# Two-tile experts with six units of lag in one shared pair buffer, four units converted ahead, and copies of turned rows ahead of conversions

## The chip, the cores and the metric

The kernel runs on one core of a Trainium2 chip. The metric is the device time of one execution in microseconds (us), taken as the median of several runs. Engines are called as in the profile: PE is TensorE (PEld its weight loads, PEldq the part of PE that reads the program in order and puts weight loads and matmuls into its queue, here called the sequencer), DVE is VectorE, ACT is ScalarE, POOL is GpSimd, SP is SyncE.

## What is computed

Three layers follow one another, all in float32: a retention attention over 8 heads (2 x 768 tokens), a dense layer of two matmuls with a leaky maximum between them (512 to 2048 to 512), and a layer of eight experts, in which each of the 1536 tokens goes to one expert. The change touches the third layer alone:

```python
def _moe2_ref(x, w_gate, w1, w2, capacity):
    N, D = x.shape                        # 1536, 512
    E = w_gate.shape[1]                   # 8
    logits = x @ w_gate
    expert_idx = np.argmax(logits, axis=1)
    ...
    disp = np.zeros((E, capacity, D), dtype=np.float32)    # capacity 384
    for i in range(N):
        e = expert_idx[i]
        if counts[e] < capacity:
            disp[e, counts[e]] = x[i]
            pos[i] = counts[e]
            counts[e] += 1
            keep[i] = True
    h = np.maximum(np.einsum('ecd,edf->ecf', disp, w1), 0.0)
    y = np.einsum('ecf,efd->ecd', h, w2)
    for i in range(N):
        if keep[i]:
            out[i] = gate_w[i] * y[expert_idx[i], pos[i]]
```

## The kernel before, in words

**The stage that the change touches.** The attention and the dense layer fill the span up to about 346 us, the experts the rest. The experts run one after the other. Each expert's 1024 hidden columns are cut into `PF` = 8 units of 128. A unit `u` holds 512 KB of weights: its part of w1 (columns 0 to 511 of the buffer) and its part of w2 (columns 512 to 1023). `refill` loads a unit's buffer (`land`, `xland`) on SP's queue long before its use.

**Classes.** How many tokens an expert has is known only at run time. `by_class` compares the count in a register with 128 and 256 and branches, so the program holds the code of an expert three times: for one, two or three tiles of 128 tokens. With the inputs of this case the eight experts have 144, 384, 35, 77, 80, 27, 183 and 384 tokens; so experts 0 and 6 are of class 2, experts 1 and 7 of class 3, and experts 2 to 5 of class 1. At the end of an expert every engine branches to the code of the next one's class (L1080 and L1081). `name_next` (L838) tells the sequencer ahead of time which way the first of these branches goes.

**One expert.** `expert` runs over steps `i`. In a step it computes the hidden columns of unit `i` on PE (`mm_h`: for classes 2 and 3 twelve matmuls, since each float32 operand stands as a high and a low part; for class 1 four matmuls on the operands as they are). `ew_h` then takes the relu from PSUM: ACT writes the high part `gh` (L746), DVE the low part `gl` (L747). `mm_y` (L756) multiplies the hidden columns of unit `i - lag` with w2 and sums in PSUM: three matmuls for a tile of tokens. `LAGS` says how many units the hidden columns are ahead of these products: 8, 4 and 2 for classes 1, 2 and 3.

**Conversions.** `conv` makes the high part (`hi`, ACT, L726) and the low part (`lo`, DVE, L727) of a unit's weights. For class 1 only the w2 half is needed (128x512), for the other classes both halves (128x1024). The list `todo` holds what is converted during an expert: its own units but the first two, which were converted in the expert before it (four ahead of expert 0), and at the end the first two of the next expert, at full width because the next class isn't known yet. A conversion is issued behind each `ew_h`, as far as buffers are free.

**The next expert's rows.** `load_x` gathers an expert's token rows by an indirect DMA on POOL. `prep_x` turns them: PE transposes into PSUM (L653), then ACT and DVE copy them to SBUF as high and low parts (`cxh`, L656, and `cxl`, L660), or for class 1 as plain halves (`cxf`, L664 and L671). In step `PREP[cls]` (8, 5, 4) the turn is issued first, then the next gather, then `mm_h`, `mm_y` and the conversion of that step, and the copies last. All of it goes through `by_class`, since the next expert's class decides the number of tiles.

## Time and profile before

| what | value |
|---|---|
| median of 3 runs | 539.44 us (537.92 to 539.96) |
| the profiled execution's own time | 537.16 us |
| its span in the profile | 535.4 us |
| PE busy (matmuls) | 514.8 us, 96% of the span |
| DVE busy | 329.4 us, 62% |
| ACT busy | 234.2 us, 44% |
| POOL busy | 39.5 us, 7% |
| mean granted clock of PE | 0.99 |

The span runs from the first instruction to the last; 1.76 us of the profiled execution's time lie around it. The shares are means over stages. PE's matmuls are pipelined, so two of them overlap in the records and a group's distance from start to start is what it costs, not its duration.

### The profile page before, as it was taken

The numbers are of one execution on the slowest core, as the hardware profiler recorded it, in microseconds if no ns is written. First come the engines' busy times: TensorE is split into PE (matmuls) and PEld (weight loads), VectorE is DVE, ScalarE is ACT, GpSimd is POOL, SyncE is SP. The second block draws the span as 40 slices with busy tenths as digits, with TensorE's granted clock in tenths as the row PEclk, the third lists the DMA queues.
The fourth block names the chain that finished last, engine by engine and source line by source line (L and its number), as shares of the span: only waits on it lengthen the run. The fifth ranks groups of instructions, "written<-read, shape, count | busy, mean of one in ns | idle before, by whom it ended". The sixth has DMA issues, their size and how long they took to land.

```text
span 535.4 us, 8754 instructions
## 1 busy us (share of the span) xinstructions
PE 514.8 (96%) x3279; PEld 460.2 (86%) x3281; DVE 329.4 (62%) x636; ACT 234.2 (44%) x485; POOL 39.5 (7%) x66
## 2 busy tenths in 40 slices
PE   7899999999999999999999999899799999998995
PEld 4888989999999999999999998588798899986894
DVE  3999993379689649947735254553343666655430
ACT  1887973354344325423422231252333566654421
POOL 0000000000000000000001012411101212201002
PEclk9999999999999999999999999989899999999998
DMA  8987781022334602410411313463451999910001
GB/s 318 376 271 253 238 260 58 1 80 78 99 105 151 196 2 78 122 38 5 153 65 75 137 59 119 134 227 103 111 164 46 372 339 354 366 72 13 21 1 60
DMA packets 23783, 76.54 MB, mean 143 GB/s; under 512 B 3578, under 2 KB 3706, under 8 KB 23712
## 3 DMA queue, kind: packets, MB, share of 16 engines
q1 hardware_dynamic: 21312, 70.26, 37.9%
q0 software_dynamic: 2400, 5.39, 2.9%
q8 instruction: 38, 0.62, 0.5%
q14 instruction: 33, 0.27, 0.2%
HBM read 68.15 MB, written 9.96 MB: 146 GB/s over the span
## 4 chain that ended last, share of the span: by engine, by line
PE 61%; DMA 24%; issue 10%; DVE 2%; POOL 1%; ACT 1%; POOLq 1%; DVEq 0%
PE ps_h L369 25%; DMA xr<-x2d,gix 24%; PE ps_y L420 18%; PE ps_a L420 7%; PE ps_a L251 2%; PE ps_a L185 2%; PE ps_a L469 2%; PE ps_a L240 2%; PE ps_a L456 1%; PE ps_h L223 1%; PE ps_y L888 1%; DVE am L207 0%; POOL xr L638 0%; POOL out L850 0%; PE ps_a L597 0%
## 5 line engine op out<-in xcount | busy, mean ns | idle before, releaser
L376 ACT ACTIVATE hs<-ps_h 128x384 f32<-128x384 f32 x64 | 31.4, 490 | 106.0 <-PE ps_h L369 106.0
L381 DVE SCALAR_TENSOR_TENSOR hs<-hs 128x384 f32<-128x384 f32 x64 | 35.6, 556 | 67.5 <-ACT hs L376 67.5
L420 PE MATMUL ps_y<-hi,gh 128*128 128x512 f32 x138 | 56.3, 408 | 0.0
L369 PE MATMUL ps_h<-xh,hi 128*128 128x384 f32 x256 | 55.7, 339 | 0.0
L369 PE MATMUL ps_h<-xl,hi 128*128 128x384 f32 x256 | 54.8, 336 | 0.0
L369 PE MATMUL ps_h<-xh,lo 128*128 128x384 f32 x256 | 54.7, 336 | 0.0
L420 PE MATMUL ps_y<-lo,gh 128*128 128x512 f32 x138 | 54.0, 391 | 0.0
L420 PE MATMUL ps_y<-hi,gl 128*128 128x512 f32 x138 | 54.0, 391 | 0.0
L385 ACT ACTIVATE gh<-hs 128x384 fp32r<-128x384 f32 x64 | 33.6, 526 | 45.0 <-DVE hs L381 45.0
L369 PEld LDWEIGHTS ps_h<-xh,hi 128*128 128x128 f32 x256 | 46.0, 188 | 4.8
L391 DVE TENSOR_TENSOR gl<-hs,gh 128x384 fp32r<-128x384 f32 x64 | 35.6, 556 | 21.3 <-ACT gh L385 21.3
L747 DVE SCALAR_TENSOR_TENSOR gl<-ps_h,gh 128x384 fp32r<-128x384 f32 (+2 forms) x44 | 18.5, 421 | 48.7 <-ACT gh L746 41.8
L369 PEld LDWEIGHTS ps_h<-xl,hi 128*128 128x128 f32 x256 | 45.3, 188 | 0.0
L369 PEld LDWEIGHTS ps_h<-xh,lo 128*128 128x128 f32 x256 | 45.0, 188 | 0.0
L756 PE MATMUL ps_y<-hi,gh 128*128 128x512 f32 x112 | 44.2, 395 | 0.0
L756 PE MATMUL ps_y<-hi,gl 128*128 128x512 f32 x112 | 43.9, 392 | 0.0
L756 PE MATMUL ps_y<-lo,gh 128*128 128x512 f32 x112 | 43.8, 391 | 0.0
L746 ACT ACTIVATE gh<-ps_h 128x384 fp32r<-128x384 f32 (+2 forms) x44 | 16.9, 385 | 56.8 <-PE ps_h L705 45.2
L727 DVE TENSOR_TENSOR lo<-xland,hi 128x1024 fp32r<-128x1024 f32 (+1 forms) x32 | 32.7, 1023 | 9.3 <-ACT hi L726 9.1
L727 DVE TENSOR_TENSOR lo<-land,hi 128x1024 fp32r<-128x1024 f32 (+1 forms) x28 | 27.9, 995 | 8.5 <-ACT hi L726 6.1
L420 PEld LDWEIGHTS ps_y<-hi,gl 128*128 128x128 f32 x138 | 25.9, 188 | 5.6
L420 PEld LDWEIGHTS ps_y<-hi,gh 128*128 128x128 f32 x138 | 26.0, 188 | 4.3 <-issue 0.3
(162 smaller groups left out, 964.9 us busy)
## 6 DMA issues: line engine op xcount, KB each, us to landing
land<-wc SPq DMA_DIRECT2D x32, 512.0 KB, 4.3
xland<-wc SPq DMA_DIRECT2D x32, 512.0 KB, 4.3
land<-wb SPq DMA_DIRECT2D x31, 512.0 KB, 5.0
land<-qkv SPq DMA_DIRECT2D x19, 512.0 KB, 5.6
out<-zero SPq DMA_DIRECT2D x12, 256.0 KB, 6.4
x2d<-rows SPq DMA_DIRECT2D x12, 256.0 KB, 2.1
early<-qkv SPq DMA_DIRECT2D x5, 512.0 KB
cst<-cst_in SPq DMA_DIRECT2D x1, 512.0 KB
```

Of the source, the lines that this page charges most:

```text
L185: nc.tensor.matmul(out=at["s", c][h2][:, a, :], lhsT=kT[r, a, :], rhs=qT[r, a, :], start=True, stop=True)
L240: nc.tensor.matmul(out=y_ps[:, a, :], lhsT=at["t", c - 1][:, a, :], rhs=at["q", c][:, a, :], start=(a == 0), stop=False, skip_group_check= ...
L369: nc.tensor.matmul(out=h_ps, lhsT=w[i][:, dc * P:(dc + 1) * P], rhs=x[j][:, dc, :], start=(n == 0), stop=(n == 3 * KD - 1))
L376: nc.scalar.activation(out=hs, in_=gt[u][0], func=ACTF.Copy)
L381: nc.vector.scalar_tensor_tensor(out=hs, in0=hs, scalar=0.01, in1=hs, op0=ALU.mult, op1=ALU.max)
L385: nc.scalar.activation(out=gh, in_=gt[u][0], func=ACTF.Copy)
L391: nc.vector.tensor_tensor(out=gl, in0=hs, in1=gh.bitcast(F32), op=ALU.subtract)
L420: nc.tensor.matmul(out=yb[ti][t], lhsT=gt[u][i][:, t * P:(t + 1) * P], rhs=w[j][:, 512:1024], start=(f == fs[0] and n == 0), stop=(f == fs ...
L727: nc.vector.tensor_tensor(out=lo[:, o], in0=src[:, o], in1=hi[:, o].bitcast(F32), op=ALU.subtract)
L746: nc.scalar.activation(out=gh, in_=hp, func=ACTF.Relu)
L747: nc.vector.scalar_tensor_tensor(out=gl, in0=hp, scalar=0.0, in1=gh.bitcast(F32), op0=ALU.max, op1=ALU.subtract)
L756: nc.tensor.matmul(out=yps[t], lhsT=gg[i][:, t * P:(t + 1) * P], rhs=w[j][:, 512:1024], start=(k == 0 and n == 0), stop=(k == PF - 1 and n ...
```

## The change

Five things are changed in the expert stage:

1. **Buffers.** The relu's outputs of all classes (and the pairs of the dense layer, which come earlier) live in one tile `pairs`, cut by class: 8 pairs of 128 columns, 6 of 256 (the last three quarter-buffers in a tile `more` that reuses the dense layer's `sums`), or 4 of 384. `h_of` uses all free PSUM banks of a class.
2. **Lag.** Class 2 runs six units ahead instead of four (`LAGS`).
3. **`AHEAD`.** Four units of the next expert are converted during an expert, at full width, instead of two.
4. **Place of the copies.** The copies of the turned rows are issued right behind the turn and the gather, ahead of the step's `mm_h`, `mm_y` and conversion. `PREP` becomes 8, 8, 5 and `NAME` 4, 8, 8.
5. **Form of the branches in `prep_x`.** The first tile is turned without a question; a second and a third inside nested `If`s without an `Else`. The copies are asked in two nested steps.

```diff
@@ -94,7 +94,9 @@
-    g_p = ctx.enter_context(tc.tile_pool(name="g", bufs=3))
+    g_p = ctx.enter_context(tc.tile_pool(name="g", bufs=1))
+    pairs = g_p.tile([P, 6 * BW], FR, name="pairs")
+    sums = g_p.tile([P, 2 * BW], F32, tag="sums", name="hs")
...
@@ -659,35 +666,47 @@
-        def high(cls):
-            if cls == 1:
-                nc.scalar.activation(out=f[:, 0:2, :], in_=tps[0][:, 0:2, :], func=ACTF.Copy)
-                return
-            for t in range(cls):
+        def high(ts):
+            for t in ts:
                 hi1(t)
 
-        def low(cls):
-            if cls == 1:
-                nc.vector.tensor_copy(out=f[:, 2:KD, :], in_=tps[0][:, 2:KD, :])
-                return
-            for t in range(cls):
+        def low(ts):
+            for t in ts:
                 lo1(t)
...
-        by_class(s, 0, lambda cls: [turn(t) for t in range(cls)])
+        def half(e):
+            if e == ENGS[1]:
+                nc.scalar.activation(out=f[:, 0:2, :], in_=tps[0][:, 0:2, :], func=ACTF.Copy)
+            else:
+                nc.vector.tensor_copy(out=f[:, 2:KD, :], in_=tps[0][:, 2:KD, :])
+
+        turn(0)
+        with tc.If(over(s, ENGS[0], 1)):
+            turn(1)
+            with tc.If(over(s, ENGS[0], 2)):
+                turn(2)
         yield
-        by_class(s, 1, high)
-        by_class(s, 2, low)
+        for e, fn in ((ENGS[1], high), (ENGS[2], low)):
+            with tc.If(over(s, e, 1)) as many:
+                fn((0, 1))
+                with tc.If(over(s, e, 2)):
+                    fn((2,))
+            with many.Else():
+                half(e)
         yield
...
@@ -726,19 +744,25 @@
-    LAGS = {1: PF, 2: 4, 3: 2}
-    PREP = {1: 8, 2: 5, 3: 4}
-    NAME = {1: 4, 2: 9, 3: 8}
+    LAGS = {1: PF, 2: 6, 3: 2}
+    PREP = {1: 8, 2: 8, 3: 5}
+    NAME = {1: 4, 2: 8, 3: 8}
+    AHEAD = 4
     every = []
 
     def h_of(u, cls):
-        banks = (hps + yps[cls:])[:5 - cls]
+        banks = hps + yps[cls:]
         i = u % PF // len(banks) % (4 // (cls + cls % 2))
         return banks[u % PF % len(banks)][:, i * cls * P:(i + 1) * cls * P]
 
+    more = []
+
     def g_of(u, cls):
-        i = u // 4 % 2 if cls == 1 else 0
-        return [x[:, i * P:(i + cls) * P] for x in gpair[u % 4]]
+        i = u % PF % {1: 8, 2: 6, 3: 4}[cls]
+        w = cls * P
+        n = 6 * BW // w
+        return [pairs[:, j * w:(j + 1) * w] if j < n else more[0][:, (j - n) * w:(j - n + 1) * w]
+                for j in (2 * i, 2 * i + 1)]
...
@@ -764,8 +788,8 @@
-        todo = [(u, cls) for u in range(u0 + (4 if s == 0 else 2), u0 + PF)]
-        todo += [(u, 2) for u in range(u0 + PF, min(NU, u0 + PF + 2))]
+        todo = [(u, cls) for u in range(u0 + AHEAD, u0 + PF)]
+        todo += [(u, 2) for u in range(u0 + PF, min(NU, u0 + PF + AHEAD))]
...
@@ -800,6 +823,7 @@
                 step(xg)
                 if s + 2 < NS:
                     load_x(s + 2)
+                step(xg)
             h = hidden(i) if i < PF else None
...
-            if i == PREP[cls] and xg is not None:
-                finish_all(xg)
             refills(i)
```

The first place at which instructions move is PE's program in a class 1 expert, at the turn of the next expert's rows, between its hidden columns and its first products. Before, the turn stands there three times, once for each class; these are the copies for two tiles and for one, and the products behind them (the rows are in the program's order; which of them run is decided by the branches):

```order
L629 COMPARE_AND_BRANCH
L653 MATMUL ps_a<-cst,xr 128x128 [waits DMASW3_49]
L653 MATMUL ps_a<-cst,xr 128x128 x3
L653 MATMUL ps_a<-cst,xr 128x128 [waits DMASW4_49,DMASW6_49,DMASW2_49,DMASW0_49]
L653 MATMUL ps_a<-cst,xr 128x128 x3
L629 UNCONDITIONAL_BRANCH
L653 MATMUL ps_a<-cst,xr 128x128 [waits DMASW3_49]
L653 MATMUL ps_a<-cst,xr 128x128 x3
L629 UNCONDITIONAL_BRANCH
L756 MATMUL ps_y<-hi,gh 128x512 [waits Activation_49]
L756 MATMUL ps_y<-lo,gh 128x512
L756 MATMUL ps_y<-hi,gl 128x512
```

In the changed kernel the same place reads:

```order
L660 MATMUL ps_a<-cst,xr 128x128 [waits DMASW3_49]
L660 MATMUL ps_a<-cst,xr 128x128 x3
L698 COMPARE_AND_BRANCH
L660 MATMUL ps_a<-cst,xr 128x128 [waits DMASW4_49,DMASW6_49,DMASW2_49,DMASW0_49]
L660 MATMUL ps_a<-cst,xr 128x128 x3
L700 COMPARE_AND_BRANCH
L660 MATMUL ps_a<-cst,xr 128x128 [waits DMASW7_49,DMASW5_49,DMASW1_49]
L660 MATMUL ps_a<-cst,xr 128x128 x3
L700 UNCONDITIONAL_BRANCH
L700 UNCONDITIONAL_BRANCH [waits PE_49]
L698 UNCONDITIONAL_BRANCH [waits PE_49]
L780 MATMUL ps_y<-hi,pairs 128x512 [waits Activation_49]
```

The turn of one tile stands once, ahead of the question. On the side of an `If` that does nothing there is now a branch that waits for PE's own semaphore (`PE_49`, which PE's matmuls raise when they are done), that is, for the transposes just issued. It is run through where the next expert is of class 1 (the row with L698) and where it is of class 2 (L700), not where it is of class 3.

The second place is DVE's program at the end of a class 1 expert. Before (`gl` is the relu's low part, `lo` a converted weight, `cxl` and `cxf` copies of turned rows):

```order
L727 TENSOR_TENSOR lo<-xland,hi 128x1024 [waits DMAHW4_49,Activation_49]
L626 COMPARE_AND_BRANCH
L660 TENSOR_TENSOR cxl<-ps_a,cxh 128x4x128 [waits Activation_49,Pool_49]
L660 TENSOR_TENSOR cxl<-ps_a,cxh 128x4x128 x2
L626 UNCONDITIONAL_BRANCH
L629 COMPARE_AND_BRANCH
L660 TENSOR_TENSOR cxl<-ps_a,cxh 128x4x128 [waits Activation_49,Pool_49]
L660 TENSOR_TENSOR cxl<-ps_a,cxh 128x4x128
L629 UNCONDITIONAL_BRANCH
L671 COPY cxf<-ps_a 128x256 [waits Activation_49]
L629 UNCONDITIONAL_BRANCH
L727 TENSOR_TENSOR lo<-xland,hi 128x1024 [waits DMAHW5_49,DVE_49,Activation_49]
```

In the changed kernel:

```order
L706 COMPARE_AND_BRANCH
L667 TENSOR_TENSOR cxl<-ps_a,cxh 128x4x128 [waits PE_49]
L706 UNCONDITIONAL_BRANCH
L706 UNCONDITIONAL_BRANCH [waits DVE_49]
L695 COPY cxf<-ps_a 128x256 [waits PE_49,Activation_49]
L704 UNCONDITIONAL_BRANCH
L745 TENSOR_TENSOR lo<-xland,hi 128x1024 [waits DMAHW4_49,DVE_49,Activation_49]
L745 TENSOR_TENSOR lo<-xland,hi 128x1024 [waits DMAHW5_49,DVE_49,Activation_49]
L745 TENSOR_TENSOR lo<-xland,hi 128x1024 [waits DMAHW6_49,DVE_49,Activation_49]
L745 TENSOR_TENSOR lo<-xland,hi 128x1024 [waits DMAHW7_49,DVE_49,Activation_49]
L1101 UNCONDITIONAL_BRANCH
```

The copy now stands ahead of all conversions, and four conversions of full width follow it in a row where two stood before, one of them ahead of the copies. In both kernels the third unit of a following class 1 expert waits on PE for the last of these conversions.

## Rows read from the trace of the kernel before

**Rows 1.** The page's first part: busy us, share of the span, instructions.

```profile
PE 514.8 (96%) x3279; PEld 460.2 (86%) x3281; DVE 329.4 (62%) x636; ACT 234.2 (44%) x485; POOL 39.5 (7%) x66
```

**Rows 2.** Stretches: us, busy time (count) of each engine, granted clock, DMA share, GB/s.

```profile
466.80:476.20 9.40, 8.19 (x61) 7.36 (x60) 5.92 (x9) 6.01 (x9) 1.03 (x1) 1.00 0.44 174
```

**Rows 3.** Timeline of PE, expert 0: start, us, instruction group, idle before.

```profile
355.64 0.63 PE L705 MATMUL ps_h<-cxh,hi 128*128 128x256 f32 x4
...
358.47 0.40 PE L756 MATMUL ps_y<-hi,gh 128*128 128x512 f32 x1
```

**Rows 4.** Timeline of PE, first five units of expert 6.

```profile
466.82 0.63 PE L705 MATMUL ps_h<-cxh,hi 128*128 128x256 f32 x4
...
471.21 0.74 PE L705 MATMUL ps_y<-cxh,lo 128*128 128x256 f32 x4 [0.52 <-DVE lo L727]
...
475.16 0.74 PE L705 MATMUL ps_h<-cxh,lo 128*128 128x256 f32 x4 [0.52 <-DVE lo L727]
...
476.21 0.40 PE L756 MATMUL ps_y<-hi,gh 128*128 128x512 f32 x1
```

**Rows 5.** Timelines of ACT and of DVE, the same stretch.

```profile
470.18 1.05 ACT L726 ACTIVATE hi<-land 128x1024 fp32r<-128x1024 f32 x1
...
469.93 1.23 DVE L727 TENSOR_TENSOR lo<-land,hi 128x1024 fp32r<-128x1024 f32 x1 [0.52 <-ACT hi L726]
471.07 0.42 DVE L747 SCALAR_TENSOR_TENSOR gl<-ps_h,gh 128x256 fp32r<-128x256 f32 x1
```

**Rows 6.** Timeline of PE, turn and products of expert 4, start of expert 5.

```profile
447.37 0.60 PE L653 MATMUL ps_a<-cst,xr 128*128 128x128 f32 x4
447.72 0.48 PE L756 MATMUL ps_y<-hi,gh 128*128 128x512 f32 x1
...
453.30 1.95 PE L699 MATMUL ps_h<-cxf,xland 128*128 128x128 f32 x16
455.08 0.39 PE L699 MATMUL ps_y<-cxf,xland 128*128 128x128 f32 x2
```

**Rows 7.** PE's sequencer, single lines: duration ns min/median/max, first and last start.

```profile
L653 PEldq EVENT_SEMAPHORE  x1: 51/51/51, 446.1 to 446.1; - x1
...
L1080 PEldq COMPARE_BRANCH  x1: 2425/2425/2425, 436.1 to 436.1; - x1
L1080 PEldq COMPARE_BRANCH  x1: 2585/2585/2585, 449.2 to 449.2; - x1
...
L629 PEldq COMPARE_BRANCH  x6: 75/222/226, 389.1 to 459.3; - x6
```

**Rows 8.** The same columns, the two branches into expert 7, and PE's timeline there.

```profile
L1081 PEldq COMPARE_BRANCH  x1: 3266/3266/3266, 488.7 to 488.7; - x1
L1081 PEldq COMPARE_BRANCH  x1: 3477/3477/3477, 492.2 to 492.2; - x1
...
488.70 0.39 PE L756 MATMUL ps_y<-hi,gh 128*128 128x512 f32 x1
...
495.83 0.94 PE L705 MATMUL ps_h<-cxh,hi 128*128 128x384 f32 x4 [2.84 <-issue]
496.61 0.86 PE L705 MATMUL ps_h<-cxh,lo 128*128 128x384 f32 x4
...
498.00 0.86 PE L705 MATMUL ps_h<-cxh,hi 128*128 128x384 f32 x4
```

**Rows 9.** Timeline of PE, start of expert 1.

```profile
377.93 1.62 PE L705 MATMUL ps_h<-cxh,hi 128*128 128x384 f32 x4 [2.67 <-issue]
...
381.65 0.85 PE L705 MATMUL ps_h<-cxh,hi 128*128 128x384 f32 x4
```

**Rows 10.** Timelines of ACT and of DVE, end of expert 4.

```profile
448.70 1.06 ACT L726 ACTIVATE hi<-xland 128x1024 fp32r<-128x1024 f32 x1 [0.85 <-PE ps_y L756]
...
451.27 1.22 DVE L727 TENSOR_TENSOR lo<-xland,hi 128x1024 fp32r<-128x1024 f32 x1
454.91 0.29 DVE L747 SCALAR_TENSOR_TENSOR gl<-ps_h,gh 128x128 fp32r<-128x128 f32 x1 [2.42 <-ACT og L847]
```

More of the change, by code (lines that the diff above doesn't have):

```diff
@@ L372, in h_sum @@
         gt[u] = [h_ps]
+    order_of = {}
     def h_copy(u):
-        hs = g_p.tile([P, BW], F32, name="hs", bufs=2)
+        n = order_of.setdefault(u, len(order_of))
+        hs = sums[:, n % 2 * BW:(n % 2 + 1) * BW]
         nc.scalar.activation(out=hs, in_=gt[u][0], func=ACTF.Copy)
@@ L383, in h_high @@
     def h_high(u):
-        gh = g_p.tile([P, BW], FR, name="gh")
+        n = order_of[u] % 3
+        gh = pairs[:, n * BW:(n + 1) * BW]
         nc.scalar.activation(out=gh, in_=gt[u][0], func=ACTF.Copy)
@@ L389, in h_low @@
         hs, gh = gt[u]
-        gl = g_p.tile([P, BW], FR, name="gl")
+        n = order_of[u] % 3
+        gl = pairs[:, (3 + n) * BW:(4 + n) * BW]
         nc.vector.tensor_tensor(out=gl, in0=hs, in1=gh.bitcast(F32), op=ALU.subtract)
@@ L660, in lo1, with one @@
             nc.vector.tensor_tensor(out=l[:, :, tok], in0=tps[t], in1=h[:, :, tok].bitcast(F32), op=ALU.subtract)
-        def high(cls):
-            if cls == 1:
-                nc.scalar.activation(out=f[:, 0:2, :], in_=tps[0][:, 0:2, :], func=ACTF.Copy)
-                return
-            for t in range(cls):
-                hi1(t)
-        def low(cls):
-            if cls == 1:
-                nc.vector.tensor_copy(out=f[:, 2:KD, :], in_=tps[0][:, 2:KD, :])
-                return
-            for t in range(cls):
+        def high(ts):
+            for t in ts:
+                hi1(t)
+        def low(ts):
+            for t in ts:
                 lo1(t)
+        def one():
+            nc.scalar.activation(out=f[:, 0:2, :], in_=tps[0][:, 0:2, :], func=ACTF.Copy)
+            nc.vector.tensor_copy(out=f[:, 2:KD, :], in_=tps[0][:, 2:KD, :])
         if known:
@@ L679, in prep_x @@
                 if known == 1:
-                    high(1)
-                    low(1)
+                    one()
                 else:
@@ L685, in prep_x @@
             return
[L687 to L690 removed]
+        def half(e):
+            if e == ENGS[1]:
+                nc.scalar.activation(out=f[:, 0:2, :], in_=tps[0][:, 0:2, :], func=ACTF.Copy)
+            else:
+                nc.vector.tensor_copy(out=f[:, 2:KD, :], in_=tps[0][:, 2:KD, :])
+        turn(0)
[3 more added lines that the diff above has]
+                turn(2)
+        yield
+        for e, fn in ((ENGS[1], high), (ENGS[2], low)):
[5 more added lines that the diff above has]
+                half(e)
         yield
@@ L1068, in retention_moe_moe_kernel @@
         load_counts()
-        gpair.extend((g_p.tile([P, BW], FR, name="gh"), g_p.tile([P, BW], FR, name="gl")) for _ in range(3))
-        gpair.append([g_p.tile([P, BW], FR, tag="hs", name=n, bufs=2) for n in ("gh", "gl")])
+        more.append(g_p.tile([P, 2 * BW], FR, tag="sums", name="more"))
         for _ in range(2):
```

2 lines of the change are left out of this document (removed).

## The prediction

> **What bounds the kernel now.** I read the page first: PE is busy for 96% of the span, no other engine for more than 62% [rows 1]. A change can only help by closing gaps of PE, or hurt by opening some. So next came PE's timeline over the expert stage, for every idle entry and every group of matmuls longer than its kind. The reader should find three sorts.
>
> First, the start of expert 6. Its five hidden units before the first product take from 466.82 to 476.21, 9.39 us [rows 4]. In expert 0, same class and shapes, two such units take 355.64 to 358.47, so 1.415 each [rows 3]; five would take 7.08. The loss is **2.31 us**, and the stretch has 8.19 us of busy PE in 9.40, partly in lengthened groups [rows 2]. The entries name DVE's `lo` at L727 as what came late [rows 4]. ACT needs 1.05 us for a unit's high part, DVE 1.23 for its low part plus 0.42 for the relu's [rows 5]: 1.65 of DVE work a unit against 1.415 on PE, with each conversion issued only one or two units ahead of its use. Expert 0 doesn't suffer: it has four units converted ahead.
>
> Second, the way into the two class 3 experts: PE idles 2.67 us ahead of 377.93 and 2.84 ahead of 495.83, both put down to "issue" [rows 8, 9]. There the sequencer runs two branches of about 3.3 us one behind the other [rows 8]. It comes to the first at 488.7 while PE starts the product of 488.70; PE ends at 495.83 - 2.84 = 492.99, and at 0.229 us a product (below) that is a lead of 18 to 19 products, 4.3 us, against 488.7 to 495.8 in branches. Behind the first gap the clock is lower: four matmul groups start over 3.72 us where three warm ones of the same shape take 3 x (498.00 - 496.61) / 2 = 2.09 [rows 8, 9], so the gap costs another 1.6.
>
> Third, the exits of class 1 experts. The sequencer meets the same sort of branch for 2.43 or 2.59 us [rows 7], but PE has no gap there: products go on to 453.30 while the branch of 449.2 ends at 451.8 [rows 6, 7]. The slack is 1.5 us.
>
> **The change, part by part.** The sum is made against the profiled execution, 537.16 us, which is 2.28 under the median of the runs shown; its change is then added to that median.
>
> *Four units converted ahead* removes the first loss: when expert 6 starts, units 0 to 3 are ready, and units 4 and 5 are used 4 x 1.415 = 5.7 us and later after its start, while DVE has done the conversion of unit 4 some 1.4 + 0.4 + 1.05 + 1.23 = 4.1 us after it (a unit, the relu's high part put at its low part's 0.4, and the conversion). **-2.31**, bounds 0 (something else late in the same place) and -2.31. Expert 0 had this already. Classes 1 and 3 have no such idle entry at their start, so nothing more is to be had there.
>
> What it adds lies in the tail of the expert before: two more full conversions, and in class 1 experts at full width where half was enough. DVE's last conversion of expert 4 ends at 451.27 + 1.22 = 452.49, and it then idles 2.42 us [rows 10]; two more need 2.44. Expert 5's third unit waits for the last of them; its first starts at 453.30, the third 1.78 later at 455.08 [rows 6]. With the one-tile copies ahead of the conversions and the first at 448.70 + 0.4 (ACT must wait for a product's end, which the next paragraph shifts), the chain is 449.1 + 1.06 + 4 x 1.22 = 455.0 against 455.08 + 0.4 = 455.5. It fits by 0.5 us: I take 0, upper bound 0.4 for each of the four boundaries behind experts 2 to 5.
>
> *The branch that waits for the transposes.* Before, the sequencer reaches the turn of expert 4 at 446.1, 1.3 us ahead of PE at 447.37, and goes on issuing products; the first starts 0.35 us after the first transpose, inside the 0.60 us of the four [rows 6, 7]. In the changed kernel no product is issued until the transposes have raised the semaphore. So the product starts at 0.60 at the earliest instead of 0.35: +0.25 at least. To it come the wake-up and the branch itself; the nearest row is L629, 0.075 to 0.226 us [rows 7]; and the first group behind a wait takes 0.74 instead of 0.63 [rows 4], +0.11. Upper bound 0.25 + 0.23 + 0.11 = 0.59, rounded to 0.65 for the wake-up; I take 0.4, nearer to the short branch, because the waiting row stands directly ahead of the code that it goes on to. It is run in experts 1 to 4 (next is class 1) and 5 (next is class 2): 5 x 0.4 = **+2.0**, bounds 1.25 and 3.25. Queued behind it on PE is everything: the expert's 24 products. Who waits for these is ACT (conversions into freed buffers, the output's scaling), 0.4 later each.
>
> [...]
>
> *The lead lost by it.* After the wait the sequencer starts level with PE. It took 446.1 to 449.2 for 28 matmuls, 0.11 each [rows 7]; PE needs (453.30 - 447.72)/24 = 0.23 for a product [rows 6]. After 24 products at 0.11 it is at the exit branch 2.64 later, with 24 x 0.23 - 2.64 = 2.9 us of work queued, against 2.59 for the branch. I take 0; upper bound 0.6 at each of three exits, from the longest branch shown, 3.48 [rows 8].
>
> *Lag 6, buffers, banks, `PREP`, `NAME`.* Class 2's six units are six pairs in `pairs` and `more`, and PE does the same matmuls in another order: 0. The cover is DVE's and ACT's idle time (5.92 and 6.01 busy of 9.40 [rows 2]); were it gone, the loss would be that of expert 6 again, 2.3. The turn of the class 2 experts moves behind the second product group, with 36 products (8.2 us) behind it for the copies. Removed copies of the turn shorten the program but no executed row: 0. Copies ahead of conversions: 0, they are used only in the next expert. SP's and POOL's queues get the same issues in the same order.
>
> Sum: -2.31 + 2.0 = **-0.3**; 537.16 becomes 536.85, and the median 539.44 becomes **539.1**. By the bounds: -2.31 + 1.25 = -1.1, and -2.31 + 3.25 + 4 x 0.4 + 3 x 0.6 = +4.3.
>
> **The rivals.**
>
> *A: the wait costs next to nothing,* because the sequencer wakes within the transposes' tail. Then -2.3: 537.1. For it: PE's shown ends overlap, so 0.60 may be too long. Against: 0.52 us of idle behind a late `lo` shows that a wait is seen on PE at once [rows 4].
>
> *B: the way into class 3 gets shorter.* With lag 6, 36 to 42 products instead of 30 stand behind the last hidden unit of a class 2 expert; if the sequencer used that to get further ahead, the gaps of 2.67 and 2.84 would shrink and the clock's 1.6 come back: up to -7.1 more, 532. Against: at 488.7 it was 18 or 19 products ahead though 30 stood there [rows 8], which looks like a limit of the queue. [...]
>
> *C: the emptied sequencer doesn't get its lead back before the exits* (slower). If it has only 8 products in the queue when a branch of 2.59 begins, PE idles 2.59 - 1.84 = 0.75 at each of four exits: +3.0, and the sum is +2.7: 542.1. With a fallen clock behind one gap, 1.6 more: 543.7. It decides from about 12 products queued (2.76 us) downwards. For it: the lead is the only cover of these branches. Against: 0.11 us an instruction leaves 2.9.
>
> *D: the change doesn't do what it says:* expert 6 still waits, because the conversions of its units come late from their other side (a buffer not yet free in expert 5). Then +2.0: 541.4. Against: DVE idles at the end of each class 1 expert [rows 10].
>
> **How the numbers follow.** Forecast (between -1.1 and +1.0 of the median) 0.55, A 0.13, B 0.09, C 0.15, D 0.08. About 2.7 us, 0.5%, is what a measurement of this kernel can tell from none; the three runs shown spread over 2.0. Faster by that: B, half of A (a little more gained anywhere), and some of the forecast's noise, 0.22. Slower: most of C and a third of D, 0.17. Within: 0.61. Range: from 536.6, which takes in A, to 542.0, which takes in D and reaches to C; outside are B and C with a fallen clock.
>
> **What would show it.** Right: expert 6's first hidden units at 1.415 us each without an idle entry put down to `lo`; in experts 1 to 5 an idle entry or a later first product behind the transposes, 0.6 to 1.0 after the first one instead of 0.35; the same gaps into experts 1 and 7. Wrong: class 1 exits with an "issue" gap (C), a third unit of a class 1 expert that waits for `lo` (the conversions' chain), or gaps into class 3 under 2 us (B).

## The result and the profile after

The changed kernel is slower: 545.9 us (median of 4, 544.16 to 547.57) against 539.12 (median of 4, 537.92 to 539.96), a ratio of 1.0127 with a 95% interval of 1.0089 to 1.0166. Its profiled execution took 547.57 us, span 545.7; that is the slowest of its four, and the one of before (537.16) lies under all four of its own, so the two traces lie 10.3 us apart where the medians lie 6.8 apart.

The page's first part answers to [rows 1]:

```profile
PE 517.1 (95%) x3279; PEld 462.3 (85%) x3281; DVE 334.2 (61%) x636; ACT 238.9 (44%) x485; POOL 39.0 (7%) x66
```

PE has as many matmuls as before; most of the 10.3 us is idle. Cut at the first hidden matmul of each expert in PE's timeline, the two traces compare so (us, start of an expert to the start of the next, of expert 7 to its last product):

```
expert          0      1      2      3      4      5      6      7
before      28.14  35.51  13.68  13.11  13.07  13.52  29.02  33.29
after       32.88  36.28  13.54  13.49  16.35  15.89  26.52  32.94
difference  +4.74  +0.77  -0.14  +0.38  +3.28  +2.37  -2.50  -0.35
```

The stage ahead of expert 0 is 1.74 longer too. The change moves only the dense layer's buffers there, and changed kernels with the same code there reach expert 0 between 349.4 us (experiment 15) and 351.5, so this is taken as scatter. PE's timeline of after, in the stretches of [rows 9], [rows 6] and [rows 3, 4]: start, us, group, idle before.

```profile
384.41 1.62 PE L724 MATMUL ps_h<-cxh,hi 128*128 128x384 f32 x4 [7.45 <-issue]
...
454.86 0.60 PE L660 MATMUL ps_a<-cst,xr 128*128 128x128 f32 x4
455.61 0.47 PE L780 MATMUL ps_y<-hi,pairs 128*128 128x512 f32 x1
...
460.94 0.40 PE L780 MATMUL ps_y<-hi,pairs 128*128 128x512 f32 x1
464.07 3.63 PE L718 MATMUL ps_h<-cxf,xland 128*128 128x128 f32 x16 [2.74 <-issue]
467.50 2.02 PE L718 MATMUL ps_y<-cxf,xland 128*128 128x128 f32 x16
...
472.92 1.04 PE L660 MATMUL ps_a<-cst,xr 128*128 128x128 f32 x8
474.39 0.50 PE L780 MATMUL ps_y<-hi,pairs 128*128 128x512 f32 x1 [0.43 <-ACT cxh L663]
...
479.97 0.63 PE L724 MATMUL ps_h<-cxh,hi 128*128 128x256 f32 x4
...
489.89 0.39 PE L780 MATMUL ps_y<-hi,pairs 128*128 128x512 f32 x1
```

Read it from the bottom. In expert 6 seven units now stand before the first product, 489.89 - 479.97 = 9.92 us: 7 x 1.417, the pitch of [rows 3], and no idle entry. The stall is gone. In expert 4 the first product starts 0.75 after the first transpose (experts 1 to 4 alike), 0.40 more than in [rows 6]. In expert 5 it is 1.47, against 0.79 in the trace of before (the starts are rounded), 0.68 more:

```profile
460.44 1.04 PE L653 MATMUL ps_a<-cst,xr 128*128 128x128 f32 x8
461.24 0.48 PE L756 MATMUL ps_y<-hi,gh 128*128 128x512 f32 x1
```

All that was expected in kind. Not expected: PE idles 7.45 us ahead of expert 1 (2.67 in [rows 9]), and 2.74 ahead of expert 5, where there was no gap.

PE's sequencer, the branches at the ends of experts, answers to [rows 7, 8]: duration in ns, first and last start. The first four are those into experts 1 and 7; L1101 are the exits of experts 2, 3 and 4.

```profile
L1102 PEldq COMPARE_BRANCH  x1: 5309/5309/5309, 372.7 to 372.7; - x1
L1102 PEldq COMPARE_BRANCH  x1: 6037/6037/6037, 378.2 to 378.2; - x1
...
L1102 PEldq COMPARE_BRANCH  x1: 3672/3672/3672, 499.5 to 499.5; - x1
L1102 PEldq COMPARE_BRANCH  x1: 2928/2928/2928, 503.4 to 503.4; - x1
...
L1101 PEldq COMPARE_BRANCH  x1: 871/871/871, 430.1 to 430.1; - x1
L1101 PEldq COMPARE_BRANCH  x1: 1394/1394/1394, 443.6 to 443.6; - x1
L1101 PEldq COMPARE_BRANCH  x1: 6722/6722/6722, 457.1 to 457.1; - x1
```

Into expert 1 the two take 11.35 us; in the trace of before they took 3.50 and 3.06:

```profile
L1081 PEldq COMPARE_BRANCH  x1: 3502/3502/3502, 371.0 to 371.0; - x1
L1081 PEldq COMPARE_BRANCH  x1: 3063/3063/3063, 374.7 to 374.7; - x1
```

The sum grew by 4.78, exactly what the gap grew by. The exit of expert 4 takes 6.72 against 2.59 in [rows 7]; that of expert 3 is shorter than before (1.39 against 2.43).

The lengths of these branches go with packets in the list of DMA packets. q8, a queue of kind `instruction`, has 38 of them in the trace of before and 39 in that of after, all of 16 KB. Behind the one of 90.62 us seven more start up to 265.53 in the trace of before, while PE runs 892 matmuls and 891 weight loads: 255 a packet. So they are taken as PE's code here, and a block as 256 instructions, an estimate from that count. From that list and the sequencer's records (start and duration of the branches, us; start of the code packets; the position is that of the branch's target in its block of 256 instructions, counted from the start of the compiled program without its labels, which are marks and no instructions):

```
second branch into 1     branch         code packets      position
before             374.70 + 3.06    375.24                      41
after              378.21 + 6.04    380.19, 381.86             205
exit of expert 4
before             449.20 + 2.59    449.45                      77
after              457.08 + 6.72    461.29                     157
exits of experts 2 and 3, after
                   430.14 + 0.87    428.70                     107
                   443.61 + 1.39    442.66                       4
```

In these two traces a branch ends 1.3 to 1.5 us after its last packet has landed (0.9 to 1.4 us a packet). The second branch into expert 1 now needs two packets; the exit of expert 4 gets its one only 4.2 us after the branch began. The last two rows show what a short exit is: its packet started 1.4 and 0.95 us ahead of the branch, so much of the wait was over when the branch came (they end 1.35 and 1.39 us after it landed, as the others do). Windows of after: us, busy time (count) of PE, PEld, DVE, ACT, POOL, granted clock, DMA share, GB/s.

```profile
372.70:375.70 3.00, 3.00 (x15) 2.46 (x14) 1.55 (x2) 0.00 (x0) 0.00 (x0) 1.00 0.74 220
463.90:467.10 3.20, 3.02 (x15) 3.06 (x16) 0.39 (x2) 0.80 (x2) 0.00 (x0) 0.55 0.20 68
```

The first is the stretch from the first branch into expert 1 to its packet's start, 3.00 us with DMA at 0.74 (two refills of 512 KB issued by SP). In the trace of before it is 0.95 us at 0.23:

```profile
371.00:371.95 0.95, 0.95 (x6) 0.79 (x5) 0.00 (x0) 0.00 (x0) 0.00 (x0) 1.00 0.23 78
```

The second shows what this gap costs behind it: the granted clock is 0.55 (1.00 in the trace of before from 453.30 to 455.10), and expert 5's first sixteen matmuls take 467.50 - 464.07 = 3.43 where [rows 6] has 1.78. So the exit of expert 4 costs 2.74 + 1.65 = 4.4 in this execution. Not every gap had that behind it: at the start of expert 1 the clock was 0.50 behind 7.45 us of idle (0.54 behind 2.67 in the trace of before), at that of expert 7 it was 1.00 behind 2.70 (1.00 behind 2.84).

Theories after this, tested below: the code's position in its blocks decides how many packets a branch needs and when the late one comes (layout); refills that come free at an expert's end, four at once by the conversions run ahead, hold back the code's packets (refills); the sequencer's lost lead (rival C); and work that the change moved, such as the gathers or the copies.

### The profile page after: what moved, and what is told of

It is laid out like the page before. It is cut to its first block, busy times and chain, and to the rows that moved or that the text cites. A ratio compares the mean times of both kernels' runs of the same rounds, so it can differ in the third digit from the quotient of the medians.

```text
span 545.7 us, 8754 instructions
## 1 busy us (share of the span) xinstructions
PE 517.1 (95%) x3279; PEld 462.3 (85%) x3281; DVE 334.2 (61%) x636; ACT 238.9 (44%) x485; POOL 39.0 (7%) x66
## 5 line engine op out<-in xcount | busy, mean ns | idle before, releaser
L427 PE MATMUL ps_y<-hi,pairs 128*128 128x512 f32 x276 | 97.1, 400 | 0.0
L780 PE MATMUL ps_y<-hi,pairs 128*128 128x512 f32 x188 | 62.7, 394 | 0.9 <-ACT cxh L663 0.4
L427 PEld LDWEIGHTS ps_y<-hi,pairs 128*128 128x128 f32 x276 | 51.9, 188 | 9.9 <-issue 0.3
L427 PE MATMUL ps_y<-lo,pairs 128*128 128x512 f32 x138 | 54.0, 391 | 0.0
L391 ACT ACTIVATE pairs<-hs 128x384 fp32r<-128x384 f32 x64 | 33.6, 526 | 45.1 <-DVE hs L386 45.1
L398 DVE TENSOR_TENSOR pairs<-hs,pairs 128x384 fp32r<-128x384 f32 x64 | 35.7, 558 | 21.3 <-ACT pairs L391 21.3
L771 DVE SCALAR_TENSOR_TENSOR pairs<-ps_h,pairs 128x128 fp32r<-128x128 f32 (+2 forms) x38 | 15.5, 408 | 49.2 <-ACT pairs L770 47.1
L780 PEld LDWEIGHTS ps_y<-hi,pairs 128*128 128x128 f32 x188 | 35.3, 188 | 8.7 <-ACT pairs L770 1.1
L770 ACT ACTIVATE pairs<-ps_h 128x128 fp32r<-128x128 f32 (+2 forms) x40 | 14.9, 374 | 57.8 <-PE ps_h L724 38.3
L780 PE MATMUL ps_y<-lo,pairs 128*128 128x512 f32 x96 | 37.5, 391 | 0.0
L427 PE MATMUL ps_a<-hi,pairs 128*128 128x512 f32 x108 | 36.3, 390 | 0.0
L724 PE MATMUL ps_h<-cxh,hi 128*128 128x384 f32 (+1 forms) x112 | 23.5, 335 | 11.0 <-issue 10.1
L745 DVE TENSOR_TENSOR lo<-land,hi 128x1024 fp32r<-128x1024 f32 (+1 forms) x28 | 29.5, 1071 | 6.5 <-ACT hi L744 6.3
```

What stands on the lines that cost most here:

```text
L391: nc.scalar.activation(out=gh, in_=gt[u][0], func=ACTF.Copy)
L398: nc.vector.tensor_tensor(out=gl, in0=hs, in1=gh.bitcast(F32), op=ALU.subtract)
L427: nc.tensor.matmul(out=yb[ti][t], lhsT=gt[u][i][:, t * P:(t + 1) * P], rhs=w[j][:, 512:1024], start=(f == fs[0] and n == 0), stop=(f == fs ...
L724: nc.tensor.matmul(out=hp, lhsT=w[i][:, dc * P:(dc + 1) * P], rhs=(h, l)[j][:, dc, 0:cls * P], start=(n == 0), stop=(n == 3 * KD - 1))
L745: nc.vector.tensor_tensor(out=lo[:, o], in0=src[:, o], in1=hi[:, o].bitcast(F32), op=ALU.subtract)
L770: nc.scalar.activation(out=gh, in_=hp, func=ACTF.Relu)
```

## Experiments

Medians are us of the slowest core; the kernel before was timed in the same jobs: 539.59 beside experiments 1 to 4, 539.22 beside 5 to 8, 539.15 beside 9 to 12 and 538.16 beside 13 to 15. Kernels of different jobs are compared by their ratio to it. The expectations of experiments 9 and 10 count positions with jumps that the compiled program leaves out, up to 62 of them: their 219, 59, 117 and 213 are 205, 45, 55 and 151 in the compiled program, which is the count used here.

**1. The turn as before.** Of the changed kernel only PE's form of the turn goes back.

```diff
-        turn(0)
-        with tc.If(over(s, ENGS[0], 1)):
-            turn(1)
-            with tc.If(over(s, ENGS[0], 2)):
-                turn(2)
+        by_class(s, 0, lambda cls: [turn(t) for t in range(cls)])
```

> The changed kernel with the turn asked class by class again, so that no branch on PE waits for the transposes. Theory T (the branches into the next expert's code are slow because their code fetch shares the DMA engines with weight refills that the change moved there): the five waits of 0.40 us go, 2.0 in all, and the gap into expert 1 stays at 6 to 8 us; the time falls from 545.9 to 542.5 to 545, the more if the lead of PE's queue hides an exit of class 1 again. Rival W (the waits on PE and the lead lost by them are the cause): back to 536 to 538. Rival L (the layout of the code or the earlier hint makes the branches slow): as T, and the gap into expert 7 is long too.

Measured: 538.2 (536.6 to 540.19, 10 runs), 0.9982 [0.996, 1.0004]. The turn's 0.35 is back, the exit of expert 4 has no gap, and expert 6 takes 26.78. Into expert 1 PE still idles 4.46. The branches there, and the exit of expert 4:

```profile
L1098 PEldq COMPARE_BRANCH  x1: 4660/4660/4660, 372.2 to 372.2; - x1
L1098 PEldq COMPARE_BRANCH  x1: 3704/3704/3704, 377.0 to 377.0; - x1
...
L1097 PEldq COMPARE_BRANCH  x1: 2766/2766/2766, 452.5 to 452.5; - x1
```

The time misses theory T (542.5 to 545) and comes 0.2 us over what rival W gave. So the nested branches carry the whole loss, 7.7 us by the medians, of which the waits at the turn are 2.3; and without them the gap into expert 1 is still 1.8 over that of before.

**2. Two units ahead**, four for expert 0 as before.

```diff
-    AHEAD = 4
+    AHEAD = 2
...
-        todo = [(u, cls) for u in range(u0 + AHEAD, u0 + PF)]
+        todo = [(u, cls) for u in range(u0 + (4 if s == 0 else AHEAD), u0 + PF)]
```

> The changed kernel with two units converted ahead instead of four (four for expert 0, as before), nothing else. Theory T: refills of only two units, not four, are free to start at the end of an expert; the gap into expert 1 falls from 7.45 to 2.5 to 4 us, the loss of 2.3 us at the start of expert 6 comes back, the time is 541.5 to 544. Rival W: the gap into expert 1 has no such wait ahead of it and stays, time 546 to 549. Rival L: the gap stays at 6 to 8 us, time 546 to 549.

Measured: 548.34 (547.96 to 549.17, 4), 1.0173 [1.0124, 1.0222]. Expert 6 takes 29.90: the stall is back, +3.4. The gap into expert 1 is 5.91; the branch at the exit of expert 4 takes 5859 ns, with a gap of 1.88. Theory T is out. So four units ahead help, and neither gap is their doing alone.

**3. Four ahead in the kernel before**, copies where they were, behind the conversions.

```diff
-        todo = [(u, cls) for u in range(u0 + (4 if s == 0 else 2), u0 + PF)]
-        todo += [(u, 2) for u in range(u0 + PF, min(NU, u0 + PF + 2))]
+        todo = [(u, cls) for u in range(u0 + 4, u0 + PF)]
+        todo += [(u, 2) for u in range(u0 + PF, min(NU, u0 + PF + 4))]
```

> The kernel before with four units converted ahead instead of two, nothing else. Theory T: the gap into expert 1 grows from 2.67 to 5 to 8 us, the 2.3 us at the start of expert 6 are saved, the time is 539 + 2 to 5 - 2.3 = 539 to 543. Rivals W and L: the gap into expert 1 stays at 2.7, the time is 536.5 to 537.5.

Measured: 543.64 (541.57 to 545.25, 10), 1.0079 [1.0052, 1.0107]. The gap into expert 1 is 4.48, without any change of the turn. And expert 6 begins with another stall, in PE's timeline:

```profile
472.33 0.78 PE L705 MATMUL ps_h<-cxh,hi 128*128 128x256 f32 x4 [3.28 <-DVE cxl L660]
```

The copies of the turned rows now stand behind four conversions and come late. That is what the fourth part of the change, copies first, is needed for.

**4. No refills at the exit of expert 0.** The first four refills that expert 1's code issues are left out; they would have brought units 23 to 26, which experts 2 and 3 use.

```diff
-        if u < NU:
+        if u < NU and not PF + LAND + XLAND <= u < PF + 4 + LAND + XLAND:
```

> The changed kernel without the first four weight refills of expert 1's code, those that start between 372 and 378 us; the units that would have come in by them are computed with stale weights. Theory T: the two branches into expert 1 take 3 to 3.5 us each as those into expert 7, the gap there is 2.5 to 3.3 us instead of 7.45, the time 545.9 - 4 to 5 = 541 to 542. Rivals W and L: the gap stays at 6 to 8 us, the time within 1 us of 545.9.

Measured: 543.38 (543.17 to 547.49, 7), 1.0087 [1.0046, 1.0128]. The first branch into expert 1 takes 3765 ns instead of 5309, the second 5177 with its two packets; the gap is 5.04 instead of 7.45. The exit of expert 4 stays at 5895. So the refills hold back the first branch, and explain neither the second packet nor expert 4. They aren't all that holds it back: its packet starts 1.49 us after the branch although no other packet moved until then. By the medians the time falls by 2.5, not by the 4 to 5 of theory T.

**5. Refills held** (kernel of experiment 1, and the refills of classes 2 and 3 begin with an expert's fifth unit rather than its first; all are made).

```diff
+            if s and cls > 1:
+                if k == 0:
+                    return
+                if k == 1:
+                    refill(u0 + AHEAD + LAND + XLAND)
...
-                refill(filled[0] + LAND + XLAND)
+                if not (s and cls > 1 and filled[0] == u0 + AHEAD):
+                    refill(filled[0] + LAND + XLAND)
```

> As e1 (no branch on PE that waits for the transposes), and in classes 2 and 3 the refills of an expert begin only with its fifth unit, so that they start after PE has entered it and not at the exit of the expert before. If refills at the exit are what lengthens the branches into expert 1 (theory T): the gap there falls from 4.6 in e1 to 2.5 to 3.3 us, and the time from 538.2 to 536 to 537.5. If not: the gap stays at 4 to 6, the time at 537.5 to 539.

Measured: 536.81 (535.92 to 537.3, 5), 0.9945 [0.9928, 0.9962]. The gap into expert 1 is 2.70, as before the change. The branches, and the window from the first one to its packet:

```profile
L1104 PEldq COMPARE_BRANCH  x1: 3250/3250/3250, 372.2 to 372.2; - x1
L1104 PEldq COMPARE_BRANCH  x1: 3352/3352/3352, 375.6 to 375.6; - x1
```

```profile
372.17:373.12 0.95, 0.95 (x6) 0.79 (x5) 0.95 (x2) 0.00 (x0) 0.00 (x0) 1.00 0.00 0
```

Here, with the DMA engines idle, the packet starts 0.95 us after the branch, as in the trace of before; in the changed kernel, behind refills, 3.00.

**6. One gather for expert 6** instead of two, so that the second half of its rows is left out; the second gather is in flight at the exit of expert 4.

```diff
-        by_class(s, 3, lambda c: [gather(t) for t in range(c)])
+        by_class(s, 3, lambda c: [gather(t) for t in range(1 if s == 6 else c)])
```

> The changed kernel with one gather instead of two for expert 6, which is issued in expert 4; the second half of expert 6's rows is stale. Theory G: in the three profiles with the waits on PE the exit branch of expert 4 began when POOL had issued this second gather and its code fetch started 3.4 to 4.2 us later, in the three without them it began 0.4 us ahead of the gather and the fetch started at once; so without that gather the branch takes 0.4 to 2.8 us instead of 5.9 to 6.7, the gap into expert 5 is 0 instead of 2 to 2.9, the low clock behind it goes, and the time falls by 4 to 5 from 545.9 to 541 to 542. Rival (the lead or the layout of the code): the branch still takes 5 to 7 us, the time stays within 1 us.

Measured: 544.54 (542.28 to 548.48, 4), 1.0101 [1.0044, 1.0157]; the branch at the exit of expert 4 still takes 5955 ns. The gather is not the cause.

**7. The nested branches in the kernel before**, on PE alone.

```diff
-        by_class(s, 0, lambda cls: [turn(t) for t in range(cls)])
+        turn(0)
+        with tc.If(over(s, ENGS[0], 1)):
+            turn(1)
+            with tc.If(over(s, ENGS[0], 2)):
+                turn(2)
```

> The kernel before with the turn in nested Ifs without an Else, nothing else. Theory W (these waits are most of the loss): each of the turns in experts 1 to 4 takes 0.75 instead of 0.35 us to the next matmul and that in expert 5 1.47 instead of 0.79, 2.3 us in all, and the exit of expert 4 comes to lie behind the second gather, 2 to 5 us more with the clock; 541.5 to 546.5. Rival (only together with the other parts): 541 to 542 with no gap into expert 5.

Measured: 542.83 (541.76 to 546.52, 6), 1.0082 [1.0047, 1.0117]. The turns are 0.75 and 1.46 (0.90 in expert 1), as in the changed kernel. The exit of expert 4 takes 2550 ns, without a gap; into expert 1 the branches take 3284 and 5107, the second with two packets, and the gap is 4.55. So the wait at the turn doesn't produce the gap at expert 4's exit, and the form of the turn does bring the second packet.

**8. `PREP` and `NAME` as before** in the kernel of experiment 1.

```diff
-    PREP = {1: 8, 2: 8, 3: 5}
-    NAME = {1: 4, 2: 8, 3: 8}
+    PREP = {1: 8, 2: 5, 3: 4}
+    NAME = {1: 4, 2: 9, 3: 8}
```

> As e1, with the steps of the turn and of the hint as before (5 and 9 in class 2, 4 in class 3). If the late turn and gather in expert 0 are what lengthens the way into expert 1: the gap there falls from 4.6 to 2.5 to 3.3, the time is 536 to 537.5. If not: gap 4 to 6, time 537.5 to 539.

Measured: 537.9 (535.99 to 539.43, 9), 0.9973 [0.9948, 0.9999]: no difference in time that can be told from experiment 1, and the prediction had none for these two. The gap into expert 1 is 2.88 here instead of 4.46, as the first theory has it, so in these two traces the steps of the turn and of the hint bear on the way into expert 1; the time doesn't show it.

**9. The changed kernel with 96 instructions more that never run.** Class 1 code of expert 0, whose class is 2, gets six units twice; all code behind it moves by 96 places.

```diff
+            if s == 0 and cls == 1:
+                for _ in range(1 if k < 6 else 0):
+                    mm_h(u, cls)
```

> The changed kernel with 24 more matmuls in expert 0's code for one tile, which never runs with these inputs: what runs is the same, but PE's code from expert 1 on lies 96 instructions further. Theory L (where the branch's target lies in a block of 256 instructions, 16 KB, the size of one code fetch: by a count of PE's instructions it is 219 into expert 1 in the kernels whose branch there took two fetches, and 55 to 59 in those with one): one fetch into expert 1, the second branch there 3 to 4 us instead of 6.0, the gap 4 to 6 instead of 7.45; into expert 7 the target goes from 117 to 213 and the branch there takes two fetches, 4.5 to 6 us instead of 2.9, gap 4 to 5. Rival (not the layout): two fetches into expert 1, one into expert 7, gaps as before. If expert 4's exit of 6.7 us hangs on the layout too, it falls to 2 to 3 us and the time to 541 to 543; if not, it stays at 5.5 to 7 us.

Measured: 540.96 (539.4 to 541.81, 4), 1.0049 [0.9999, 1.0099]: 4.9 us faster than the changed kernel by the medians, 4.2 by the ratios to before, with more code. The second branch into expert 1 and the exit of expert 4:

```profile
L1105 PEldq COMPARE_BRANCH  x1: 3152/3152/3152, 377.7 to 377.7; - x1
...
L1104 PEldq COMPARE_BRANCH  x1: 1521/1521/1521, 453.9 to 453.9; - x1
```

One packet instead of two, position 45 instead of 205, and no gap into expert 5. Not as expected: the way into expert 7 kept one packet (3203 ns). Its target had gone to position 151, not to 213.

**10. Experiment 1 with 160 instructions more that never run** (the edit of experiment 9 with ten units). It puts the good target at the bad position, 205.

```diff
+            if s == 0 and cls == 1:
+                for _ in range(2 if k < 2 else 1):
+                    mm_h(u, cls)
```

> As e1, with 40 more matmuls in the same code that never runs, so that the branch into expert 1 has its target 219 into a block instead of 59, as in the changed kernel. Theory L: two fetches, the second branch 5 to 6 us instead of 3.7, the gap into expert 1 from 4.6 to 6 to 7.5, the time 539.5 to 541. Rival: one fetch, gap 4 to 5, time 538.

Measured: 540.8 (540.29 to 542.29, 4), 1.0054 [1.0004, 1.0103]; 2.6 slower than experiment 1. Two packets on the second branch into expert 1, as forecast, and a gap of 6.16. The second branch into expert 7 got two as well (PE idle 4.40 instead of 2.96); that was not foreseen, but it fits: its target stands at position 224 here. Over all 17 traces the second branches into experts 1 and 7 took two packets in the eleven cases with a target at 203 to 206 or 224, and one in the 23 cases with a target at 41 to 151. This was read after the runs.

```profile
L1101 PEldq COMPARE_BRANCH  x1: 5012/5012/5012, 375.4 to 375.4; - x1
...
L1101 PEldq COMPARE_BRANCH  x1: 5030/5030/5030, 492.5 to 492.5; - x1
```

**11. The changed kernel with held refills**: the edit of experiment 5, of which this is the core.

```diff
+            if s and cls > 1:
+                if k == 0:
+                    return
```

> The changed kernel with the refills of classes 2 and 3 held back until PE has entered the expert, as e5, but with the waits on PE as in the change. Theory T: the gap into expert 1 falls from 7.45 by 1.5 to 3 us to 4.5 to 6 (two fetches stay), the exit of expert 4 stays slow, the time 542.5 to 544.5. Rival: the gap stays at 7 to 8, time 545 to 546.5.

Measured: 544.51 (542.51 to 545.68, 4), 1.0114 [1.0061, 1.0168]. The first branch into expert 1 takes 3289 ns, the second, with its two packets, 4917; the gap is 4.31. The exit of expert 4 keeps 6102. The time, 1.4 us under the changed kernel's by the medians and 0.7 by the ratios, isn't clear of noise; the branches are.

**12. Copies back behind the conversion**, in the kernel of experiment 2.

```diff
+        xg = None
...
-                step(xg)
...
+            if i == PREP[cls] and xg is not None:
+                finish_all(xg)
```

> As e2 (the changed kernel with two units ahead), with the copies of turned rows put back behind the step's conversion; PE's code has then instruction for instruction the length of that of e7, which had a quick exit of expert 4 (2.55 us) where e2 had 5.86. If the place of the copies on ACT and DVE makes that exit slow: 2 to 3 us, no gap into expert 5, time 542 to 544. If it is the lag, the buffers or the hint in PE's code: 5.5 to 7 us, gap 2, time 546 to 549.

Measured: 544.39 (543.39 to 545.67, 4), 1.0117 [1.0067, 1.0167]. The exit of expert 4 is short again:

```profile
L1103 PEldq COMPARE_BRANCH  x1: 2857/2857/2857, 452.4 to 452.4; - x1
```

By itself that would convict the copies' place. But the edit also moves code on PE by two instructions: the target of expert 4's exit goes to position 181 instead of 179. The next two kernels part the one from the other.

**13. Experiment 2 with two instructions more** (one transpose and its weight load, never run, in class 1 code of the known turn), which gives the layout of experiment 12 without its move of the copies.

```diff
+                    for _ in range(1):
+                        nc.tensor.transpose(out=tps[0][:, 0, :], in_=xr[:, 0, 0:P], identity=ident)
```

> e2 with one more transpose in expert 0's code for one tile, which never runs: PE's code lies where that of e12 lies, 2 instructions further than in e2. Theory L (where the code lies decides the exit of expert 4): the branch takes 1.5 to 3 us, no gap into expert 5, time 544 to 546 against 548.3 of e2. Rival (the place of the copies decides): 5.5 to 6.5 us, gap 2, time 547 to 549.

Measured: 544.98 (544.85 and 545.11), 1.0129 [1.0064, 1.0194].

```profile
L1103 PEldq COMPARE_BRANCH  x1: 2521/2521/2521, 454.3 to 454.3; - x1
```

**14. Experiment 12 with 254 more**, which gives it the layout of experiment 2, one block of 256 further on.

```diff
+                    for _ in range(7):
+                        nc.tensor.transpose(out=tps[0][:, 0, :], in_=xr[:, 0, 0:P], identity=ident)
...
+            if s == 0 and cls == 1:
+                for _ in range(2 if k < 7 else 1):
+                    mm_h(u, cls)
```

> e12 with 254 instructions more in code that never runs: within a block of 256 PE's code lies where that of e2 lies, the copies stay behind the conversion. Theory L: the exit branch of expert 4 takes 5.5 to 6.5 us and PE has a gap of 2 to 3 us into expert 5, time 546 to 549. Rival (the copies): 1.5 to 3 us, no gap, time 544 as e12.

Measured: 547.58 (547.35 and 547.81), 1.0177 [1.0112, 1.0243].

```profile
L1108 PEldq COMPARE_BRANCH  x1: 5926/5926/5926, 452.8 to 452.8; - x1
```

The four together (ns of the exit of expert 4; PE's gap into expert 1, us):

```
                      copies first        copies behind
exit at position 179  5859, 5.91 (exp 2)  5926, 4.45 (exp 14)
exit at position 181  2521, 6.05 (13)     2857, 4.34 (12)
```

Two instructions that are never run decide the exit of expert 4, wherever the copies stand. The copies' place decides 1.5 to 1.7 us of the gap into expert 1: there the first branch's packet starts 2.6 us after the branch with copies first (DMA share 0.65 and 0.67 until then) and 0.96 to 0.99 with copies behind (0.03 and 0.11). So "copies ahead of conversions: 0" was wrong too for this gap, though the times of the pairs differ by 0.8 us at most, and why the copies' place moves those transfers into the exit was not followed.

**15. Experiment 5 with `PREP` and `NAME` as before** (the edit of experiment 8).

> As e5 (no wait on PE, refills of classes 2 and 3 held back), with the steps of the turn and of the hint as before. In e5 the branches into expert 1 are already those without load, 3.3 us each; so the same: gap 2.5 to 3.2, time 536 to 537.5. If the late turn still costs something: 535 to 536.

Measured: 536.01 (534.85 to 536.97, 10), 0.9958 [0.9932, 0.9984]; gap into expert 1 2.83. Faster than both kernels (than the one of before by 0.4%), and not to be told from experiment 5: with the refills held, these steps make no difference.

## Why the prediction was wrong

The forecast was 539.1 us with a range of 536.6 to 542.0; 545.9 was measured.

- **Four units ahead, -2.31**: right. Expert 6 is 2.50 shorter, without an idle entry, and experiment 2 brings the stall back.
- **The wait at the turn, 5 x 0.4**: right in kind and nearly in size: 0.40 in experts 1 to 4, 0.68 in expert 5, 2.3 instead of 2.0. In experiment 7 the wait comes without the other parts. In the trace of after it is a wait of the sequencer at L698 that is over at 455.51 in expert 4, 0.65 us after the first transpose; the compiled program leaves out the jump behind it. The first product starts 0.75 after the first transpose, where the prediction had 0.60 as the least and [rows 6] has 0.35. Rival A is out.
- **The step that failed** is in the paragraph that costs the rest at nothing, "Removed copies of the turn shorten the program but no executed row: 0", and with it the expectation of "the same gaps into experts 1 and 7". The exits' branches were priced at 2.59 us, at most at the longest one shown, 3.48, and the gaps behind them at nothing; 5.3, 6.0 and 6.7 came. PE's program is 538 instructions shorter (11846 against 12384 in the compiled programs, without labels), and so every branch target stands elsewhere in its block. In this layout the second branch into expert 1 needs two packets and the exit of expert 4 gets its one late. Experiment 9 shifts the code by 96 instructions that never run, and 4.9 of the 6.8 us are gone (4.2 by the ratios); experiment 10 brings the second packet to a kernel that had one; experiments 2, 12, 13 and 14 show the exit of expert 4 turn on two instructions.
- **"SP's and POOL's queues get the same issues in the same order"**: the order is the same, the time isn't. Refills fall into the stretch in which PE waits for code. Either of two parts of the change brings it about without the other: four units ahead (experiment 3, in the kernel before: the first branch's packet 2.64 us after the branch, 0.95 without them) and copies first (experiments 2 and 13 against 14 and 12). That conversions run ahead free landing tiles earlier is argued from the code. Held back, the refills bring the first branch into expert 1 from 5309 to 3289. By the medians they return 1.4 us (experiment 1 to 5: 538.2 to 536.8; changed kernel to 11: 545.9 to 544.5); by the ratios 2.0 and 0.7, the second not clear of noise.
- **The lead.** "0.11 each" was wrong, in the harmless direction: after the wait the 24 products went through the sequencer in 455.51 to 457.08, 0.065 each. So 0.11 was not the sequencer's own pace; what held it to 0.11 before isn't shown. At 457.08 PE had products until 461.17, 4.09 us or 18 of them: the lead was whole.
- **Rival C** named the place (a class 1 exit with an "issue" gap) and the wrong mechanism. A full lead of 4.1 us doesn't cover a branch of 6.7, and experiment 7 has the waits without that gap. B and D are out: the gap into expert 7 didn't shrink (2.84 in [rows 8], 2.70 after), and expert 6 doesn't wait.

The books, by medians, with each term uncertain by 2 to 3 us (the intervals of the ratios are 0.4 to 0.5% to either side): -2.4 (the stall, 545.9 against experiment 2's 548.3), +2.3 (waits, by rows), +4.9 (layout, experiment 9), +1.4 (refills) make +6.2 against +6.8 measured. The terms are not quite independent: in the second branch into expert 1, layout and traffic act on the same packet. By rows of the two traces: 4.78 (gap into 1) + 2.3 + 4.4 (exit of 4 with its low clock) - 2.5 + 1.74 (stage ahead) = 10.7 against 10.3.

**Open**: why one position makes the fetch for the exit of expert 4 start 3.4 to 4.2 us after the branch, and another, two instructions on, within 0.5 us. Slow exits have targets at 154 to 158 and 179; quick ones at 60 to 77, 181, 225 and 253, and DMA is at about 1.0 in both. All of an expert's code moves together in these kernels, so it can't be told whether the target's place counts, or the branch's, or that of the code ahead of it. The gather (experiment 6), the units ahead (2 and 12) and the copies' place (13, 14) are excluded as the cause by themselves.

## What to carry to other kernels

In these kernels PE's queue covered some of the branches at the ends of experts only just and others not at all (4.1 us of products against 1.5 to 6.7 at the exit of expert 4), and edits that changed the count of PE's instructions, run or not, changed those branches: 96 more took the second one into expert 1 from 6037 to 3152 ns (experiment 9), two more the exit of expert 4 from 5859 to 2521 (experiment 13). With such branches in a kernel, put a price on such an edit from both sides, look for the code's packets in the trace, and compare versions with a few dozen dead instructions added before blaming what was edited. Work done earlier frees buffers earlier here (argued from the code), and the refills cost 1.4 us less by the medians when they were held back until PE had entered the expert (experiments 1 and 5). A branch on PE that waits for PE's own last matmul cost 0.4 to 0.7 us each time here; with the branches around whole alternatives in the kernel before, the product started 0.35 us after the first transpose, inside the transposes' 0.60.

## What the hardware showed

- Over all traces, a branch into another expert's code took 0.4 to 2.1 us on PE where its packet of code had started over 0.3 us ahead of it, 2.1 to 3.8 where its one packet started between 0.3 us ahead and 1.5 us after, 4.7 to 5.3 where that packet came 2.3 to 3.0 us after (at the exit of expert 0, with the kernel's own transfers under way), 4.8 to 6.0 with two packets, and 5.9 to 6.7 at the exits of expert 4 whose one packet started 3.4 to 4.2 us after.
- The DMA share alone doesn't set that start: at 1.01 and 0.70 it was 0.45 and 0.12 us after the branch (exits of expert 4 in experiments 12 and 13), at 0.74 it was 3.00 (into expert 1 in the changed kernel).
- All packets on q8 were of 16 KB, one for 255 matmuls and weight loads of PE between 90.62 and 265.53 us in the trace of before; with the target at the position of experiment 2, but 256 instructions further on, the exit of expert 4 was as slow in experiment 14 (5926 ns against 5859). In the trace of after the packets for the exits of experts 2 and 3 start 1.4 and 0.95 us ahead of the branch, that for the exit of expert 4 starts 4.2 us after it. The program's hint for these branches (`name_next`, BRANCH_PREFETCH_HINT in the trace) ran 7.7 us ahead of each of the three, at 422.45, 435.91 and 449.40.
- A second branch into expert 1 or 7 took 4.8 to 6.0 us with two packets; with one it took 2928 to 3704 ns in the traces of before and after and in experiments 1, 5 and 9.
- PE's queue held some 18 products (4.1 us) in the trace of after as in that of before, and refilled from empty at 0.065 us a product.
